# Retention and soft mixture of experts on one core: where the constant tables are fetched, and five warm-up products in place of ten

## The chip, the cores and the metric

The kernel runs on one core of a Trainium2 chip. Its engines each work through a list of their own in order: TensorE (PE; its weight loads are listed as PEld), VectorE (DVE), ScalarE (ACT), GpSimd (POOL) and SyncE (SP), and wait for one another by semaphores. A DMA is issued by an entry of an engine's list (SPq, ACTq) and moved by 16 DMA engines that all queues share. The metric is the device time of one execution in microseconds (us); a table gives the median of several runs. Times inside the kernel are from one profiled execution and count from the start of its span.

## What is computed

Two stages, all in float32. First a retention layer: for 8 batches and 8 heads of 576 positions by 64 features, scores of q and k are weighted by a decay that depends on the head and the distance, without a softmax, and multiplied by v. Then a soft mixture of experts over the 4608 rows of 512 features: logits against 32 slots, a softmax over rows to fill the slots, 8 experts of two layers on 4 slots each, and a softmax over slots to spread the result.

```python
scores = scale * np.matmul(q, k.transpose(0, 1, 3, 2))
gamma = 1.0 - 2.0 ** (-5.0 - np.arange(H, dtype=np.float32))
rel = pos[:, None] - pos[None, :]
Dmat = np.where(rel >= 0, gamma[:, None, None] ** rel[None, :, :], 0.0)
x = np.matmul(scores * Dmat[None, :, :, :], v)        # then (B*S, H*D)
logits = x @ phi
d = np.exp(logits - logits.max(0)); d /= d.sum(0) + 1e-09
slot_input = (d.T @ x).reshape(E, S_per_e, D)
for e in range(E):
    h = np.maximum(slot_input[e] @ w1[e], 0.0)
    slot_out[e] = h @ w2[e]
c = np.exp(logits - logits.max(1)); c /= c.sum(1) + 1e-09
return c @ slot_out
```

## The kernel before

The rows are cut into 36 tiles of 128 (a tile is one batch's 128 positions, all heads; the last 64 positions of two batches share a tile). The main loop runs over tiles `t`. For each there is one load of k and v (`kv`, 512 KB, four buffers) and one of q (`qs`, 256 KB, three buffers); only tile 0 gets k and v in two transfers, with q between them. The order on each engine is the order in which the code is written: `manual_schedule` lets nothing move it.

The steps of a tile, by line:

- `stage_k` (L175, L176): TensorE transposes k in four products, ScalarE copies the result to `kt`. In the loop, `stage_k(t + 1)` stands directly behind `stage_a(t)`.
- `stage_a` (L190; L195, L198): products of `kt` and q into the PSUM tile `pss`; VectorE multiplies them by masks out of the constants `cst` and writes `sT`.
- `scale` (L150, L158): GpSimd multiplies v in place by a column of `cst`, and makes `gb`, the decay table for this chunk, out of the table `g0` and `cst`.
- `stage_i` (L217): adds what earlier chunks left in the running state; the first two tiles have none.
- `stage_c` (L250, L253): k times the scaled v, into the running state.
- `stage_b` (L229, L236): scaled v times `sT` into `px`; VectorE multiplies by `gb`.

TensorE's order around the start is therefore: warm-up, `stage_k(0)`, `stage_a(0)`, `stage_k(1)`, `stage_c(0)`, `stage_b(0)`, `stage_a(1)`, `stage_k(2)` and so on. Tiles are gathered in groups of four for the softmax (L258 and further). The last part (from L566) computes the experts and writes the output.

Ahead of the loop stand the constants and the warm-up. `cst` holds masks and factors, 128 x 380 (190 KB); `g0` is 128 x 512 (256 KB). Both are issued by ScalarE, as its first two entries; SyncE issues the loads of tiles 0 to 3 at the same time, in the order k, q, v of tile 0, then k/v and q of tile 1, k/v and q of tile 2, k/v of tile 3. The warm-up is ten products of a 128 x 128 tile of zeros, `wz`, which VectorE fills first; nobody reads their result. ScalarE loads its activation table ahead of its first compute instruction, which before is the copy L176 of tile 0. `lrun` is a column that the softmax uses from the first group on, where it is first written by L282.

The semaphores of the DMAs are taken in turn, eight of them, so the issue of a later DMA can wait for an earlier one to land. The queue rows in the section on the change show which.

Of the kernel before, what the change touches and what calls it, by code (L numbers as in the profile page):

```python
# [45 lines left out]
def retention_softmoe(ctx, tc, tok, phi, wun, cst, gtab, msel, out):  # L46
    nc = tc.nc
# [25 lines left out]
    cs_ = cpool.tile([P, NCST], F32, name="cst")  # L73
# [4 lines left out]
    g0 = cpool.tile([P, NP, P], F32, name="g0")  # L78
# [7 lines left out]
    lrun = cpool.tile([P, 1], F32, name="lrun")  # L86
# [19 lines left out]
        if t < NT:  # L106
            nc.sync.dma_start(out=qs[t % NQ], in_=tok[t, :, 1024:1536])

    nc.scalar.dma_start(out=cs_, in_=cst)
    nc.scalar.dma_start(out=g0, in_=gtab)  # L110
    K, V = slice(0, 512), slice(512, 1024)
    load_kv(0, K)
    load_q(0)
# [7 lines left out]
    make_identity(nc, ident)  # L121
    wz = gpool.tile([P, P], F32, name="et")
    nc.vector.memset(wz, 0.0)
    pw = ps_x.tile([P, 2, 512], F32, name="px")
    for _ in range(10):
        nc.tensor.matmul(pw[:, 0, 0:P], lhsT=wz, rhs=wz, start=True, stop=True)  # L126

    for z in range(2):
# [347 lines left out]
    for z in range(2):  # L476
# [4 lines left out]
        if z == 0:  # L481
# [3 lines left out]
            out=acc[:, z * 256:(z + 1) * 256], in0=acc[:, z * 256:(z + 1) * 256], scalar=alpha,  # L485
# [293 lines left out]
```

## Time and profile before

| | us |
|---|---|
| median of 3 runs | 234.44 |
| lowest and highest | 233.66, 235.42 |
| profiled execution, its own time | 234.99 |
| span of the profiled execution | 233.2 |

The span goes from the first to the last instruction; the profiled execution's own time has 1.8 us more around it. The profile is read in these views: the page (busy time of each engine as a share of the span; the chain of work that ended last, followed back from the end); the timeline (start, duration, engine, line, operation, what it writes and reads, how often, and in brackets the idle time ahead of it and what ended that); the DMA issues of a stretch of time, with the time from issue to landing; the windows (busy time of engines in each stretch, with the granted TensorE clock, the busy share of the DMA engines and GB/s); the waits. A product in float32 shows as two MATMUL rows (two passes), a transpose as one. The lines themselves stand in the prediction, beside what is read from them.

### The profile page before, as it was taken

What the parts mean: (1) busy time and instruction counts of PE and PEld (TensorE: products, weight loads), DVE (VectorE), ACT (ScalarE), POOL (GpSimd) and SP (SyncE); (2) the same over time, 40 slices, a digit from 0 to 9 for tenths busy, and PEclk for the clock granted to TensorE, in tenths of its full rate; (3) what the DMA queues carried; (4) which work ended last, traced back from release to release, by engine and by line L of the source; (5) the groups of instructions that cost most, each with busy time, mean ns of one, the idle gap of its engine ahead of it and who ended that gap; (6) DMA issues with size and microseconds to landing.
All of it is one profiled execution on the core that took longest, in us unless ns stands there. A gap on an engine that the chain in (4) does not pass through costs nothing.

```text
span 233.2 us, 9102 instructions
## 1 busy us (share of the span) xinstructions
PE 216.9 (93%) x3971; PEld 159.9 (69%) x3971; DVE 131.8 (56%) x302; ACT 82.4 (35%) x198; POOL 62.5 (27%) x72
## 2 busy tenths in 40 slices
PE   8789999999999999999999999999899999999840
PEld 8678868867786886686887787887673235666530
DVE  0466647757646766845866874764664132445750
ACT  2231542442433433352253253254130142344740
POOL 2843423515314233522443441431030010000000
PEclk9999999999999999999999999999999999999995
DMA  6999899799699789889879999888202999997897
GB/s 221 393 390 317 327 350 318 279 333 371 235 337 339 262 307 402 303 266 350 299 273 359 347 366 293 302 280 288 101 0 89 357 412 405 408 393 297 356 404 311
DMA packets 23079, 72.54 MB, mean 311 GB/s; under 512 B 2560, under 2 KB 2944, under 8 KB 23040
## 3 DMA queue, kind: packets, MB, share of 16 engines
q1 hardware_dynamic: 22752, 71.51, 83.7%
q8 instruction: 31, 0.51, 0.9%
q10 hardware_dynamic: 288, 0.46, 0.6%
q14 instruction: 8, 0.07, 0.1%
HBM read 62.52 MB, written 9.44 MB: 309 GB/s over the span
## 4 chain that ended last, share of the span: by engine, by line
PE 87%; DVE 4%; ACT 2%; issue 2%; DMA 1%; DVEq 0%
PE px L229 14%; PE pss L190 13%; PE pn L258 8%; PE pst L250 7%; PE px L217 7%; PE pn L175 7%; PE pm L614 6%; PE pm L272 4%; PE pm L320 4%; PE po L639 3%; PE pst L566 3%; PE pn L566 3%; PE px L126 2%; DVE sT L195 2%; DVE sT L198 1%
## 5 line engine op out<-in xcount | busy, mean ns | idle before, releaser
L150 POOL TENSOR_TENSOR kv<-kv,cst 128x512 f32<-128x512 f32 x36 | 37.6, 1043 | 86.0 <-DMA kv<-in_tok 75.9
L236 DVE TENSOR_TENSOR x<-px,gb 128x512 f32<-128x512 f32 (+1 forms) x37 | 24.9, 675 | 30.9 <-PE px L229 30.7
L229 PE MATMUL px<-sT,kv 128*64 128x128 f32 x576 | 38.6, 275 | 2.7 <-DVE sT L198 1.9
L195 DVE TENSOR_TENSOR sT<-pss,cst 64x256 f32<-64x256 f32 x72 | 30.3, 421 | 11.9 <-PE pss L190 9.4
L176 ACT COPY kt<-pn 128x512 f32<-128x512 f32 x36 | 21.1, 588 | 42.0 <-PE pn L175 42.0
L190 PE MATMUL pss<-qs,kt 64*64 64x64 f32 (+1 forms) x1152 | 32.9, 248 | 1.4 <-ACT kt L176 0.7
L229 PEld LDWEIGHTS px<-sT,kv 128*64 128x64 f32 x576 | 30.9, 137 | 4.7 <-PE pst L250 2.4
L260 ACT COPY x<-pn 128x512 f32<-128x512 f32 x33 | 19.3, 586 | 36.5 <-PE pn L258 36.4
L190 PEld LDWEIGHTS pss<-qs,kt 64*64 64x64 f32 x1152 | 26.4, 133 | 8.4 <-issue 5.8
L250 PEld LDWEIGHTS pst<-kv 128*64 128x64 f32 x512 | 17.5, 137 | 10.1 <-issue 8.1
L175 PE MATMUL pn<-ident,kv 128*128 128x128 f32 x144 | 22.7, 280 | 0.3 <-DMA kv<-in_tok 0.3
L198 DVE TENSOR_TENSOR sT<-pss,cst 128x512 f32<-128x512 f32 x32 | 22.1, 692 | 0.9
L250 PE MATMUL pst<-kv 128*64 128x64 f32 x512 | 21.9, 228 | 0.0
L258 PE MATMUL pn<-ident,x 128*128 128x128 f32 x132 | 21.7, 287 | 0.1
L158 POOL TENSOR_TENSOR gb<-g,cst 128x512 f32<-128x512 f32 x16 | 16.7, 1041 | 12.0 <-DVE x L236 12.0
L217 PE MATMUL px<-qs,sb 64*64 64x128 f32 (+1 forms) x512 | 18.8, 267 | 0.0
L175 PEld LDWEIGHTS pn<-ident,kv 128*128 128x128 f32 x144 | 16.1, 141 | 2.1 <-DMA kv<-in_tok 0.4
L258 PEld LDWEIGHTS pn<-ident,x 128*128 128x128 f32 x132 | 13.8, 140 | 4.5 <-issue 2.8
L253 ACT COPY sb<-pst 128x256 f32<-128x256 f32 x32 | 11.7, 367 | 13.0 <-PE pst L250 12.6
L217 PEld LDWEIGHTS px<-qs,sb 64*64 64x64 f32 x512 | 12.4, 132 | 4.7 <-DVE sT L195 3.4
L601 DVE COPY ws<-po 128x512 f32<-128x512 f32 x15 | 10.1, 690 | 8.4 <-PE po L639 8.3
L599 ACT COPY ws<-po 128x512 f32<-128x512 f32 x15 | 8.7, 589 | 10.5 <-PE po L639 9.5
(143 smaller groups left out, 219.5 us busy)
## 6 DMA issues: line engine op xcount, KB each, us to landing
ws<-in_w SPq DMA_DIRECT2D x61, 512.0 KB, 6.4
kv<-in_tok SPq DMA_DIRECT2D x35, 512.0 KB, 5.5
qs<-in_tok SPq DMA_DIRECT2D x36, 256.0 KB, 4.7
out<-ws SPq DMA_DIRECT2D x14, 512.0 KB, 4.1
kv<-in_w SPq DMA_DIRECT2D x3, 512.0 KB, 4.9
out<-kv SPq DMA_DIRECT2D x3, 512.0 KB, 5.0
kv<-in_tok SPq DMA_DIRECT2D x2, 256.0 KB, 4.0
out<-ws SPq DMA_DIRECT2D x2, 256.0 KB, 6.5
```

The lines of the kernel that those rows point to most:

```text
L150: nc.gpsimd.tensor_tensor(out=v, in0=v, in1=vt[:, c, :].unsqueeze(2).broadcast_to([P, H, D]), op=ALU.mult)
L175: nc.tensor.transpose(pk[:, a, :], k[:, 2 * a:2 * a + 2, :].rearrange("p j d -> p (j d)"), ident)
L176: nc.scalar.copy(out=kt, in_=pk)
L190: nc.tensor.matmul(ps[r, j, a, cols], lhsT=kt[e, a, r], rhs=q[e, a, cols], start=True, stop=True, skip_group_check=True)
L195: nc.vector.tensor_tensor(out=s[r, :, aa, 0:64], in0=ps[r, :, aa, 0:64], in1=tri[r].unsqueeze(1).unsqueeze(2).broadcast_to([D, 2, 2, 64]), ...
L198: nc.vector.tensor_tensor(out=s[:, :, :, 64:P], in0=ps[:, :, :, 64:P], in1=gm.unsqueeze(1).broadcast_to([P, 2, NP, 64]), op=ALU.mult)
L217: nc.tensor.matmul(px[r, j, a // 2, cols], lhsT=sb[i if c == NCH else b % 2][e, a, :], rhs=qT(t)[e, a, cols], start=(i == 0 and a < 2), st ...
L229: nc.tensor.matmul(px[al * D:(al + 1) * D, j, z, :], lhsT=v[:, 2 * a + j, :], rhs=s[:, j, a, :], start=(c == 0 and z == 0), stop=True, ski ...
L236: nc.vector.tensor_tensor(out=xv[:, j], in0=px[:, j, 0:2], in1=g[:, j], op=ALU.mult)
L250: nc.tensor.matmul(pst[j * D:(j + 1) * D, a, :], lhsT=k[:, 2 * a + j, :], rhs=v[:, 2 * a + j, :], start=(c == 0 and a == 0 and b % 2 == 0) ...
L258: nc.tensor.transpose(pn[:, a, :], xT[t][:, a, :], ident)
L260: nc.scalar.copy(out=x, in_=pn)
```

## The change

The two issues of the constants move behind a new ScalarE instruction, a copy of one column of zeros into `lrun`, which waits for VectorE's fill of `wz`. The warm-up has five products in place of ten. Nothing else is changed; line numbers grow by one behind this place.

```diff
-    nc.scalar.dma_start(out=cs_, in_=cst)
-    nc.scalar.dma_start(out=g0, in_=gtab)
     K, V = slice(0, 512), slice(512, 1024)
     load_kv(0, K)
     load_q(0)
...
     wz = gpool.tile([P, P], F32, name="et")
     nc.vector.memset(wz, 0.0)
+    nc.scalar.copy(out=lrun, in_=wz[:, 0:1])
+    nc.scalar.dma_start(out=cs_, in_=cst)
+    nc.scalar.dma_start(out=g0, in_=gtab)
     pw = ps_x.tile([P, 2, 512], F32, name="px")
-    for _ in range(10):
+    for _ in range(5):
         nc.tensor.matmul(pw[:, 0, 0:P], lhsT=wz, rhs=wz, start=True, stop=True)
```

ScalarE at the program's start, before the change (`g_138` is `g0`):

```order
L109 DMA cst<-in_cst 128x380
L110 DMA g_138<-in_gtab 128x512
L176 ACT_TABLE_LOAD
L176 COPY kt<-pn 128x512 [waits PE_49]
L176 COPY kt<-pn 128x512 [waits PE_49,Activation_49]
```

And after it:

```order
L122 ACT_TABLE_LOAD
L122 COPY lrun<-et 128x1 [waits DVE_49]
L123 DMA cst<-in_cst 128x380
L124 DMA g_138<-in_gtab 128x512
L177 COPY kt<-pn 128x512 [waits PE_49]
L177 COPY kt<-pn 128x512 [waits PE_49,Activation_49]
```

The table load is now ScalarE's first entry, and both issues stand behind it and the copy.

SyncE's first issues, before (`kv_87` to `kv_90` are the buffers of k and v, `qs_91` to `qs_93` those of q, `ws` those of weights):

```order
L103 DMA kv_87<-in_tok 128x512
L107 DMA qs_91<-in_tok 128x512
L103 DMA kv_87<-in_tok 128x512
L103 DMA kv_88<-in_tok 128x1024
L107 DMA qs_92<-in_tok 128x512
L103 DMA kv_89<-in_tok 128x1024
L107 DMA qs_93<-in_tok 128x512 [waits DMAHW0_49]
L103 DMA kv_90<-in_tok 128x1024 [waits DMAHW1_49]
L107 DMA qs_91<-in_tok 128x512 [waits DMAHW3_49,DMAHW2_49,PE_49]
L97 DMA ws_96<-in_w 128x1024
L103 DMA kv_87<-in_tok 128x1024 [waits DMAHW4_49,PE_49,Pool_49]
```

And after:

```order
L103 DMA kv_87<-in_tok 128x512
L107 DMA qs_91<-in_tok 128x512
L103 DMA kv_87<-in_tok 128x512
L103 DMA kv_88<-in_tok 128x1024
L107 DMA qs_92<-in_tok 128x512
L103 DMA kv_89<-in_tok 128x1024
L107 DMA qs_93<-in_tok 128x512 [waits DMAHW0_49]
L103 DMA kv_90<-in_tok 128x1024 [waits DMAHW1_49]
L107 DMA qs_91<-in_tok 128x512 [waits DMAHW2_49,PE_49]
L97 DMA ws_96<-in_w 128x1024 [waits DMAHW3_49]
L103 DMA kv_87<-in_tok 128x1024 [waits DMAHW4_49,PE_49,Pool_49]
```

The order of the issues is the same; what has moved is which load a semaphore stands for. Before, `DMAHW0` is taken by `cst`, 1 by k, 2 by `g0`, 3 by q and 4 by v of tile 0; after, 0 by k, 1 by q, 2 by v, 3 by `cst` and 4 by `g0`.

## The prediction

> **What bounds the kernel now.** I read the page first: the busy times and the chain that ended last.
>
> ```profile
> PE 216.9 (93%) x3971; PEld 159.9 (69%) x3971; DVE 131.8 (56%) x302; ACT 82.4 (35%) x198; POOL 62.5 (27%) x72
> ...
> PE 87%; DVE 4%; ACT 2%; issue 2%; DMA 1%; DVEq 0%
> ```
>
> The kernel is bound by TensorE: 93% busy, and 87% of the chain. An edit in the first ten microseconds can therefore only make the same stream of products start earlier or later. So the second view is the timeline of the first 11 us (start, duration, engine, line).
>
> ```profile
> 0.73 0.40 ACTq L109 DMA_DIRECT2D cst<-in_cst  x1
> 0.73 0.38 SPq L103 DMA_DIRECT2D kv<-in_tok  x1
> ...
> 1.05 4.63 PE L126 MATMUL px<-et 128*128 128x128 f32 x20 [1.05 <-DVE et L123]
> 1.16 0.46 ACTq L110 DMA_DIRECT2D g<-in_gtab  x1
> ...
> 1.64 0.90 SPq L103 DMA_DIRECT2D kv<-in_tok  x2
> 1.65 1.28 ACT L176 ACT_TABLE_LOAD   x1 [1.65 <-PEq L768]
> ...
> 5.47 0.67 PE L175 MATMUL pn<-ident,kv 128*128 128x128 f32 x4
> 6.18 0.59 ACT L176 COPY kt<-pn 128x512 f32<-128x512 f32 x1 [3.25 <-PE pn L175]
> 6.68 1.04 POOL L150 TENSOR_TENSOR kv<-kv,cst 128x512 f32<-128x512 f32 x1 [4.66 <-DMA kv<-in_tok]
> ...
> 6.82 0.90 PE L190 MATMUL pss<-qs,kt 64*64 64x128 f32 x32 [0.68 <-ACT kt L176]
> ...
> 7.80 0.88 DVE L195 TENSOR_TENSOR sT<-pss,cst 64x256 f32<-64x256 f32 x2 [6.80 <-PE pss L190]
> 8.00 0.66 PE L175 MATMUL pn<-ident,kv 128*128 128x128 f32 x4 [0.28 <-DMA kv<-in_tok]
> ...
> 8.58 0.69 PE L250 MATMUL pst<-kv 128*64 128x64 f32 x16
> ...
> 8.71 0.69 DVE L198 TENSOR_TENSOR sT<-pss,cst 128x512 f32<-128x512 f32 x1
> ...
> 9.54 1.09 PE L229 MATMUL px<-sT,kv 128*64 128x128 f32 x16 [0.28 <-DVE sT L198]
> ...
> 10.57 0.90 PE L190 MATMUL pss<-qs,kt 64*64 64x128 f32 x32
> ```
>
> The reader should see two things. The k transposes of tile 0 start at 5.47, when the ten warm-up products end, with no wait of their own. And the transposes of tile 1, which stand ahead of L250 and L229 of tile 0 in TensorE's order, wait until 8.00 for a load. When each load lands is the third view: the DMA issues of narrow windows (last column: us from issue to landing), for k, cst, g0, q and v of tile 0, then k/v and q of tile 1.
>
> ```profile
> kv<-in_tok SPq DMA_DIRECT2D x1, 256.0 KB, 3.1
> cst<-in_cst ACTq DMA_DIRECT2D x1, 190.0 KB, 3.3
> ...
> g<-in_gtab ACTq DMA_DIRECT2D x1, 256.0 KB, 4.3
> qs<-in_tok SPq DMA_DIRECT2D x1, 256.0 KB, 4.2
> ...
> kv<-in_tok SPq DMA_DIRECT2D x1, 256.0 KB, 4.9
> ...
> kv<-in_tok SPq DMA_DIRECT2D x1, 512.0 KB, 5.8
> ...
> qs<-in_tok SPq DMA_DIRECT2D x1, 256.0 KB, 6.0
> ```
>
> With issues at 0.73, 0.73, 1.16, 1.17, 1.64, 2.1 and 2.6 they land at 3.8 (k), 4.0 (cst), 5.5 (g0), 5.4 (q), 6.5 (v), 7.9 (k/v of tile 1) and 8.6 (q of tile 1). So k lay ready 1.6 us before its transposes began: the warm-up was the limit there, not the load.
>
> **Five products fewer.** The ten products are 20 passes; passes start from 1.05 and the transposes follow at 5.47, 4.42/20 = 0.22 us a pass. Five products end about 1.05 + 10 x 0.22 = 3.2. By itself this frees 2.2 us of TensorE ahead of the transposes.
>
> **Constants behind the copy.** ScalarE now starts with its table load (0.73 + 1.28 = 2.0) and the one-column copy. No such copy stands in the trace; the bounds are zero and the other one-column instruction of ScalarE:
>
> ```profile
> L285 ACT ACTIVATE alpha<-mrun,negm 128x1 f32<-128x1 f32 x7 | 2.0, 281 | 0.0
> ```
>
> I take 0.2 (nearer to that row). The issue of cst moves from 0.73 to 2.2 and g0 from 1.16 to 2.6: 1.5 us later. The table load is moved, not added; before it was hidden in the 3.25 us that ScalarE idled ahead of L176. With 3.3 and 4.3 us to landing as before, cst lands at 5.5 and g0 at 6.9; with the longest time of the rows above, 6.0, at 8.2 and 8.6. I take the first: cst and g0 shared the engines evenly with k and q (3.3 beside 3.1, 4.3 beside 4.2), so they don't queue behind SyncE's loads. The first readers of cst are L195 on VectorE and L150 on GpSimd; of g0 L158 on GpSimd, behind L150. SyncE's later issues wait on semaphores that are taken in turn: q of tile 2 now waits for k instead of cst (3.4 instead of 4.0), k/v of tile 3 for q instead of k, the first weights for cst and the k/v of tile 4 for g0. The last two stand behind products of tile 0 anyway. I cost these at nothing; q of tile 2 and k/v of tile 3 queue behind the load of tile 1 and are read after 11.
>
> **k, q and v of tile 0.** cst's 190 KB and part of g0 no longer move beside k. The windows of the first transfers (last column: GB/s):
>
> ```profile
> 1.50:3.50 2.00, 2.00 (x11) 2.00 (x11) 0.00 (x0) 1.28 (x1) 0.47 (x2) 1.00 0.82 242
> 3.50:5.25 1.75, 1.75 (x10) 1.75 (x9) 0.00 (x0) 0.00 (x0) 0.00 (x0) 1.00 1.06 388
> ```
>
> At 388 GB/s 190 KB are 0.5 us, so k lands at about 3.35 (bounds: 3.83 as now, 3.3). q would land near 4.3 and v before 6.5. The transposes start at 3.4 instead of 5.47.
>
> **Where the gain stops.** Transposes at 3.4 at the slow pass rate (4 x 0.21 and a drain, about 1.1) to 4.5, L176 to 5.1, L190 from 5.2 to about 6.3 (partly slow, see below), L195 and L198 of VectorE, which took 7.80 to 9.40, now 6.4 to 8.0. sT is 1.4 us earlier. But the transposes of tile 1 still wait for kv of tile 1, and of the bytes ahead of that load none is gone: k, q, v, cst, g0 and its own 512 KB move at the same rate. So it lands at 7.9 again, the transposes stand at 8.00 and L250 at 8.58, as before. L150 of tile 0 ends by 7.6 as v lands no later, so L250 has its operand. Only then does the early sT count: L229 follows L250 at once. Before, it waited 0.28 for sT. **The sum is -0.28 us**; the other 1.1 us turn into a longer wait for the load of tile 1. Bounds of this term: the first 2 us moved 242 GB/s on two queues, 0.75 us short of 388; if one queue alone ramps at half of that and k/v of tile 1 comes 0.4 later, +0.1; if the later constants let it pass and it lands at 7.1 to 7.3 (some 250 KB of their 446 not yet moved by then: 0.6 to 0.8 us at 388 GB/s), L229 follows at 8.6 to 8.8, -0.8.
>
> Does an early start reach the end? TensorE's waits between 10 and 165 us, and GpSimd's scaling of the k/v of tile 4 against its transposes:
>
> ```profile
> PE px L229 <- DVE sT L198: 1.6, 3, 0.6
> PE pss L190 <- issue: 0.7, 2, 0.4
> ...
> 16.40 1.04 POOL L150 TENSOR_TENSOR kv<-kv,cst 128x512 f32<-128x512 f32 x1 [3.36 <-DMA kv<-in_tok]
> ...
> 18.81 0.66 PE L175 MATMUL pn<-ident,kv 128*128 128x128 f32 x4
> ```
>
> No wait for a load is among them, and tile 4's k/v is there 2.4 us ahead: a shift of under 1 us is not eaten. Near the end, with TensorE's last products ahead:
>
> ```profile
> 215.00:217.00 2.00, 1.89 (x10) 1.00 0.69 277
> ```
>
> At 215 the DMA engines are not full (0.69). The outputs that still move after TensorE's end at 224 (its rows stand below) thus start when TensorE delivers, and shift with it.
>
> **The clock, where I had to choose.** The warm-up's passes are longer than the transposes right behind them (ns, minimum, median, maximum; first and last start):
>
> ```profile
> L126 PE MATMUL px<-et x20: 421/421/579, 1.0 to 5.3; 128*128 128x128 f32 x20
> ...
> L175 PE MATMUL pn<-ident,kv x12: 272/273/341, 5.5 to 11.8; 128*128 128x128 f32 x12
> ```
>
> 421 against 273, and starts 0.21 apart against 0.11: the array ran at half rate until about 5.60, though the clock column says 1.00. TensorE's busy time in windows cut there:
>
> ```profile
> 0.99:2.19 1.20, 1.14 (x5) 1.00 0.33 54
> 2.19:5.60 3.41, 3.41 (x18) 1.00 1.03 352
> 5.60:9.01 3.41, 2.46 (x55) 1.00 0.95 363
> ...
> 224.05:227.47 3.42, 0.08 (x1) 1.00 1.02 405
> 227.47:230.88 3.41, 0.00 (x0) 0.50 1.02 405
> ```
>
> The rate rose after a stretch that was full, and fell at 227.47, 65 times 3.413 us later, after an idle one; a stretch of which 1.14 of 3.41 us were busy (33%) did not raise it. In the changed kernel the stretch 2.19 to 5.60 holds the products to 3.3, the transposes to 4.5 and L190 from 5.2: some 2.5 of 3.41 us, 73%. Whether that is enough the trace doesn't show; 73% lies 0.6 of the way from 33 to 100, and I take it that it is. Price if not: L190 at half rate (0.80 becomes 1.6) ends at 6.8, still hidden behind the load; the stretch to 9.01 is 63% busy, so it doesn't raise the clock either; then the transposes from 8.00 to 9.1, L250 1.2 to 10.3, L229 2.0 to 12.3, where now the next product stands at 10.57; the stretch to 12.43 is full. +1.8 us.
>
> The Trainium skill (TensorE: Matmul & The Clock Gate, Part 1: The HAM clock gate) says that the array's clock is released after one busy window of about 3.4 us of sustained activity, that the window runs free, and that the budget is one of time and not of products. The trace agrees on the window (65 of them) and the half rate. Read strictly, the rule speaks against this change: by it five products, 2.1 us, are too few, and the sum would be the +1.8 of the last paragraph instead of -0.28.
>
> **The rivals.**
> - *The clock rises late* (the paragraph above): 234.44 + 1.8 = 236.2. For it: the pauses ahead of 5.2 and, after 6.8, until 8.00. Against it: 73% busy. It decides from the point at which L250 and L229 of tile 0 run at half rate, so slower than before. Were tile 1 slow too, its L190, L250 and L229 would add another 1.5 to 2 and pass 1%.
> - *The constants come late.* L195 and L150 wait for cst; from a landing at 7.8 on each microsecond is lost in full. At 8.2 L150 ends at 9.3, L250 to 9.9, against 9.54 now: +0.4, 234.8. For it: the landing times grew to 6.0 with the queue; against it: the even sharing. The Trainium skill (ScalarE: Activation LUTs, What ACT_TABLE_LOAD costs) adds a drain of 1.38 us to a table load; no row here shows one, since ScalarE idled then. By it cst would land at 6.9, still ahead of 7.8, and the sum stays.
> - *The load of tile 1 comes earlier*, -0.8: 233.6. The late constants speak for it, the unchanged bytes against it.
> - *The change does nothing that can be seen*: the load of tile 1 holds L250 and L229 wherever sT is. It is my forecast less 0.28 us.
>
> **How the numbers follow.** The profiled execution took 234.99 (span 233.2 and 1.8 around it), 0.55 above the median of 234.44 in runs of 233.66 to 235.42; against it the sum gives 234.7, and against the median 234.16, so 234.2. Chances: forecast, with nothing visible, 0.50; clock late 0.30, of which 0.05 past tile 1; constants late 0.08; tile 1's load early 0.12. The range reaches from the early load with a part of the runs' spread (233.6 - 0.3 = 233.3) to the late clock with a little of it (236.3). The likeliest case alone spans 233.6 to 234.9. A measurement of this kernel tells 1%, 2.3 us, from no change: no case gains that much (0.02 for what I haven't seen), and only the clock that stays low past tile 1 loses it (0.05). Same: 0.93.
>
> **What the profile will show.** Right: L126 ends near 3.3, the transposes of tile 0 start near 3.4, sT is done near 8.0, the transposes of tile 1 wait for their load until about 8.0 with a wait of 1 us or more, L229 starts near 9.25 with no wait, and later rows stand 0.3 earlier. L126's 421 ns should be followed by passes of 273 from about 5.6 on. Wrong: L250 and L229 of tile 0 with durations near 420, or L195 or L150 waiting for cst, or the transposes of tile 1 away from 8.0.

## The result and the profile after

| | median, us | runs |
|---|---|---|
| before | 233.86 | 20 (232.17 to 235.78) |
| after | 236.28 | 20 (234.59 to 239.10) |

The ratio is 1.0091, with a 95% interval of 1.0066 to 1.0117: the change costs 2.1 us, 1.5 to 2.7. That is slower by more than the measurement is uncertain, by about 1%. The forecast of 234.2 had the wrong direction; the time lies just under the end of the range, where the rival with the late clock stood. The ratios here and below leave out executions over 1.5% above the fastest of their kernel (three of the 20 after, six of the twelve of e4), so a ratio and its two medians can differ, and in e4 they point apart.

The page of the kernel after, span, busy time, clock, and the chain that ended last:

```profile
span 232.8 us, 9083 instructions
...
PE 215.4 (93%) x3961; PEld 159.0 (68%) x3961; DVE 130.3 (56%) x302; ACT 82.7 (36%) x199; POOL 62.4 (27%) x72
...
PEclk9799999999999999999999999999999999999995
...
PE 85%; DMA 4%; DVE 3%; ACT 2%; issue 1%; SPq 1%; DVEq 0%
```

Two things are new: a 7 in the clock's second slice, and 4% of DMA in the chain. The profiled execution happens to be the fastest of its 20 (234.59), so its span must not be set against 233.2 of before; only the beginning is compared here. The timeline of the kernel after shows it:

```profile
0.73 1.28 ACT L122 ACT_TABLE_LOAD   x1 [0.73 <-PEq L769]
...
1.04 0.41 ACTq L123 DMA_DIRECT2D cst<-in_cst  x1
...
1.05 2.50 PE L127 MATMUL px<-et 128*128 128x128 f32 x10 [1.05 <-DVE et L121]
...
2.02 0.19 ACT L122 COPY lrun<-et 128x1 f32<-128x1 f32 x1
...
3.48 1.09 PE L176 MATMUL pn<-ident,kv 128*128 128x128 f32 x4
...
5.24 0.90 PE L191 MATMUL pss<-qs,kt 64*64 64x128 f32 x32 [0.67 <-ACT kt L177]
...
7.13 0.69 DVE L199 TENSOR_TENSOR sT<-pss,cst 128x512 f32<-128x512 f32 x1
...
8.23 1.08 PE L176 MATMUL pn<-ident,kv 128*128 128x128 f32 x4 [2.08 <-DMA kv<-in_tok]
...
9.23 1.12 PE L251 MATMUL pst<-kv 128*64 128x64 f32 x16
...
10.15 1.82 PE L230 MATMUL px<-sT,kv 128*64 128x128 f32 x16
...
11.89 0.90 PE L191 MATMUL pss<-qs,kt 64*64 64x128 f32 x32
```

Up to 7.8 it goes as forecast: transposes at 3.48, scores at 5.24, sT done at 7.8, and TensorE then waits 2.08 us for the load of tile 1. But the transposes behind the wait take 1.08 in place of 0.66, L251 1.12 in place of 0.69, L230 1.82 in place of 1.09. The products of tile 1 stand at 11.89, before at 10.57: 1.3 us late, not 0.3 early. These long rows of L251 and L230 are the sign that the prediction named for being wrong. The windows of the same kernel, cut where its clock changed (length, TensorE busy, clock, DMA share, GB/s), say why:

```profile
1.48:4.90 3.42, 3.09 (x14) 1.00 0.85 285
4.90:8.31 3.41, 0.98 (x33) 1.00 1.02 354
8.31:11.72 3.41, 3.41 (x36) 0.50 1.03 411
11.72:15.14 3.42, 2.80 (x66) 1.00 0.94 349
```

The clock rose at 4.90, after a window that was 90% busy. The next window, with the wait in it, was 29% busy (0.98 of 3.41), and the whole window behind it ran at half rate: exactly the one with tile 0's last products. This is one phase of the windows; the experiments show others.

### The profile page after: what moved, and what is told of

It is laid out like the page before. It is cut to its first block, busy times and chain, and to the rows that moved or that the text cites. A ratio compares the mean times of both kernels' runs of the same rounds, so it can differ in the third digit from the quotient of the medians.

```text
span 232.8 us, 9083 instructions
## 1 busy us (share of the span) xinstructions
PE 215.4 (93%) x3961; PEld 159.0 (68%) x3961; DVE 130.3 (56%) x302; ACT 82.7 (36%) x199; POOL 62.4 (27%) x72
## 4 chain that ended last, share of the span: by engine, by line
PE 85%; DMA 4%; DVE 3%; ACT 2%; issue 1%; SPq 1%; DVEq 0%
PE px L230 15%; PE pss L191 12%; PE pn L259 8%; PE pst L251 8%; PE pn L176 7%; PE px L218 7%; PE pm L615 6%; PE pm L273 4%; PE pm L321 4%; PE po L640 3%; PE pst L567 3%; PE pn L567 3%; DMA kv<-in_tok 3%; DVE sT L196 1%; DMA out<-ws 1%
## 5 line engine op out<-in xcount | busy, mean ns | idle before, releaser
L230 PE MATMUL px<-sT,kv 128*64 128x128 f32 x576 | 39.3, 279 | 2.4 <-DVE sT L199 1.6
L230 PEld LDWEIGHTS px<-sT,kv 128*64 128x64 f32 x576 | 31.7, 139 | 4.3 <-PE pst L251 2.0
L191 PE MATMUL pss<-qs,kt 64*64 64x64 f32 (+1 forms) x1152 | 31.8, 247 | 0.7 <-ACT kt L177 0.7
L176 PE MATMUL pn<-ident,kv 128*128 128x128 f32 x144 | 23.6, 289 | 2.2 <-DMA kv<-in_tok 2.1
L251 PEld LDWEIGHTS pst<-kv 128*64 128x64 f32 x512 | 17.9, 140 | 10.3 <-issue 8.4
L251 PE MATMUL pst<-kv 128*64 128x64 f32 x512 | 22.4, 231 | 0.0
L254 ACT COPY sb<-pst 128x256 f32<-128x256 f32 x32 | 11.7, 367 | 12.8 <-PE pst L251 12.3
```

The costliest lines, as they stand in the source:

```text
L176: nc.tensor.transpose(pk[:, a, :], k[:, 2 * a:2 * a + 2, :].rearrange("p j d -> p (j d)"), ident)
L191: nc.tensor.matmul(ps[r, j, a, cols], lhsT=kt[e, a, r], rhs=q[e, a, cols], start=True, stop=True, skip_group_check=True)
L230: nc.tensor.matmul(px[al * D:(al + 1) * D, j, z, :], lhsT=v[:, 2 * a + j, :], rhs=s[:, j, a, :], start=(c == 0 and z == 0), stop=True, ski ...
L251: nc.tensor.matmul(pst[j * D:(j + 1) * D, a, :], lhsT=k[:, 2 * a + j, :], rhs=v[:, 2 * a + j, :], start=(c == 0 and a == 0 and b % 2 == 0) ...
```

## The experiments

All times are medians with the ratio to the kernel before, run on the same chip. "Products of zeros" are the warm-up's own, which nobody reads; where a kernel has more of them, only idle products are added.

| run | what | median, us | before, us | ratio, 95% |
|---|---|---|---|---|
| e1 | constants moved, ten products | 234.62 | 233.65 | 1.0040 (1.0001 to 1.0078) |
| e2 | constants first, five products | 235.33 | 233.65 | 1.0083 (1.0050 to 1.0115) |
| e3 | after, and 8 products in the wait | 234.99 | 233.65 | 1.0040 (1.0001 to 1.0078) |
| e4 | after, other order of loads | 234.67 | 233.65 | 0.9969 (0.9923 to 1.0014) |
| e5 | e4 and 2 products | 233.37 | 234.02 | 0.9970 (0.9941 to 0.9999) |
| e6 | after, and 2 + 6 products | 233.13 | 234.02 | 0.9970 (0.9947 to 0.9993) |
| e7 | after, and 2 products | 234.63 | 234.02 | 1.0052 (1.0022 to 1.0082) |
| e8 | before, with 7 + 2 + 4 products | 232.77 | 234.21 | 0.9934 (0.9901 to 0.9968) |
| e9 | after with eight products | 234.67 | 234.21 | 1.0030 (0.9990 to 1.0070) |
| e10 | e8, k of tile 1 ahead | 232.41 | 233.32 | 0.9956 (0.9928 to 0.9983) |
| e11 | e8 once more | 232.96 | 233.32 | 0.9984 (0.9954 to 1.0013) |

**e1 and e2: which half of the change costs.** e1 is the changed kernel with

```diff
-    for _ in range(5):
+    for _ in range(10):
```

> The changed kernel with ten warm-up products again, so the constants' move alone. Theory A (the clock falls, or stays at half rate, because TensorE pauses for the load of tile 1): the transposes of tile 0 start at 5.5 again, the pause shrinks to under 0.5 us, the clock rises once and stays; +0.3 us against before from the later load of tile 1, at most +0.7 as an average over the phase of the clock's windows. Theory B (the moved constants make the loads of tile 1 late, and that is the loss): +1.5 to +2.5, as the whole change.

e2 is the kernel before with

```diff
-    for _ in range(10):
+    for _ in range(5):
```

> The kernel before with five products, the constants first as before. Theory A: transposes of tile 0 at about 3.9, when k lands, a pause of about 1.3 us ahead of the transposes of tile 1; half rate in a part of the executions, +0.7 to +1.3 us against before. Theory B: the load of tile 1 lands at 7.9 as before, so no loss: -0.3 to +0.2.

Measured: e1 +0.4%, 0.0 to 0.8; e2 +0.8%, 0.5 to 1.2. Five products alone, with the constants where they were, cost 1.9 us (1.2 to 2.7), nearly the whole 2.1: the loss does not need the moved constants, so theory B falls as its cause. The move alone is not cleared by this: e1's 0.9 us (0.0 to 1.8) lies between theory A's 0.3 to 0.7 and theory B's 1.5 to 2.5. e2's first stages and windows:

```profile
4.02 1.09 PE L175 MATMUL pn<-ident,kv 128*128 128x128 f32 x4 [0.47 <-DMA kv<-in_tok]
5.78 1.55 PE L190 MATMUL pss<-qs,kt 64*64 64x128 f32 x32 [0.68 <-ACT kt L176]
8.48 1.11 PE L175 MATMUL pn<-ident,kv 128*128 128x128 f32 x4 [1.14 <-DMA kv<-in_tok]
9.52 1.12 PE L250 MATMUL pst<-kv 128*64 128x64 f32 x16
10.43 1.92 PE L229 MATMUL px<-sT,kv 128*64 128x128 f32 x16
```

```profile
0.19:3.61 3.42, 2.50 (x10) 1.00 0.51 152
3.61:7.02 3.41, 2.32 (x36) 1.00 1.02 347
7.02:10.43 3.41, 2.27 (x31) 1.00 1.02 396
10.43:13.85 3.42, 3.42 (x53) 1.00 0.91 338
```

Every product is long here: scores 1.55 us in place of 0.90. Windows 73%, 68% and 67% busy did not raise the clock; it rose at 13.85, after a full one. (The clock column says 1.00 where the trace holds no clock record yet; the durations tell.) In this phase the clock never falls, it rises late.

e1's own profile fell once, after a window with the pause (1.41 of 3.42, 41%), behind a load of tile 1 that came at 9.4:

```profile
2.97:6.38 3.41, 3.41 (x17) 1.00 0.89 285
6.38:9.80 3.42, 1.41 (x36) 1.00 0.98 392
9.80:13.21 3.41, 3.41 (x41) 0.50 1.03 406
```

**e3 and e4: fill the wait, or take it away.** e3 adds to the changed kernel, behind `stage_a(0)`,

```diff
         stage_a(t)
+        if t == 0:
+            for _ in range(8):
+                nc.tensor.matmul(pw[:, 0, 0:P], lhsT=wz, rhs=wz, start=True, stop=True)
```

> The changed kernel with eight more products of zeros (read by nobody) between the scores of tile 0 and the transposes of tile 1. Theory A: the pause of 2.1 us is filled with 1.75 us at full rate, the clock rises once and stays, L251 and L230 of tile 0 run at full rate: 0.0 to +0.4 us against before, so 1.5 to 2 us of the loss are gone. Theory B: +2 stays, or more if the products run past the landing.

e4 changes the order of the loads of the changed kernel:

```diff
-    nc.scalar.dma_start(out=g0, in_=gtab)
...
-    for t in range(1, NQ):
+    load_kv(1, K)
+    nc.sync.dma_start(out=g0, in_=gtab)
+    load_q(1)
+    load_kv(1, V)
+    for t in range(2, NQ):
```

> The changed kernel with another order of loads: k of tile 1 alone (256 KB) directly behind v of tile 0, then g0 on SyncE's queue, q and v of tile 1. Both theories take the load of tile 1 for the next limit: its k should land near 6.0 and v of tile 0 near 5.5, so the pause is gone or under 0.8 us, L230 of tile 0 starts at 8 to 8.5 and the products of tile 1 at 9 to 9.6 in place of 10.57. Theory A: -1.0 to -1.5 us against before, with the clock up once in most phases. Theory B: -1.0 to -1.5 as well; if the clock falls here too, 0 to +1.

Both fell short: e3 gets back about half (+0.4%), and e4 shows no gain, where -0.4 to -0.6% was expected: its ratio is -0.3% with an interval that holds zero, and its median lies 1.0 us above that of before. The windows of e3, then of e4, show what was overlooked:

```profile
0.39:3.80 3.41, 2.54 (x11) 1.00 0.55 177
3.80:7.21 3.41, 2.74 (x37) 1.00 0.87 269
7.21:10.63 3.42, 3.42 (x17) 1.00 1.03 411
```

```profile
0.55:3.97 3.42, 2.90 (x12) 1.00 0.60 198
3.97:7.38 3.41, 2.74 (x39) 1.00 1.00 348
7.38:10.79 3.41, 3.41 (x39) 1.00 1.04 415
```

In both the clock rose only behind the third window, at 10.63 and 10.79: 80% (2.74 of 3.41) and 85% (2.90 of 3.42) do not raise it. The missing share is a hole that neither kernel filled, the 0.7 us in which TensorE waits for ScalarE's copy of k. In e3 the eight products even ran at half rate, 3.8 us, until 10.6, past the landing of tile 1's load at 8.7.

**e5, e6 and e7: fill the hole.** All three add, ahead of the loop,

```diff
     stage_k(0)
+    for _ in range(2):
+        nc.tensor.matmul(pw[:, 0, 0:P], lhsT=wz, rhs=wz, start=True, stop=True)
```

e5 to e4, e7 to the changed kernel, and e6 to the changed kernel with six products behind `stage_a(0)` as in e3.

> The kernel of e4 (other order of loads) with two more products of zeros between the transposes of tile 0 and its scores, where TensorE waited 0.7 us for the copy of k. Theory C (the clock rises only after a window of 3.41 us that TensorE fills to more than 80%, and falls after one filled to less than some 50%): TensorE is now busy without a hole from 1.05 until 7, so the clock rises by 7.4 whatever the phase, and stays. -0.8 to -1.5 us against before, all runs shifted; in the profile no half-rate product after 7.4. If five products and the pauses were not the cause, the two products cost their 0.2 us: 0 to +0.2 against e4.

> The changed kernel with two more products of zeros behind the transposes of tile 0 and six behind its scores: same loads, same order, but TensorE busy without a hole from 1.05 until the load of tile 1. Theory C: the clock rises once, by 7.4, and stays; the loss is gone: -0.2 to +0.4 us against before. If the later loads were the cause, +1.5 to +2 remain.

> The changed kernel with only the two products behind the transposes of tile 0; the pause ahead of the transposes of tile 1 stays. Theory C: the clock rises by 7.4 in every phase, and falls again in those in which a window lies mostly in the pause: +0.8 to +1.5 us against before, between e6 and the changed kernel. If only the rise mattered, as e6; if the two products did nothing, +2.1.

e6 is the clean test: its loads and their order are those of the changed kernel, its TensorE does 2.7 us more idle work (1.06 and 1.60), and the loss is gone: 0.9970, 0.9947 to 0.9993. Its first stages and windows:

```profile
5.44 0.94 PE L191 MATMUL pss<-qs,kt 64*64 64x128 f32 x32
6.31 1.60 PE L360 MATMUL px<-et 128*128 128x128 f32 x12
8.35 0.66 PE L176 MATMUL pn<-ident,kv 128*128 128x128 f32 x4 [0.44 <-DMA kv<-in_tok]
8.94 0.69 PE L251 MATMUL pst<-kv 128*64 128x64 f32 x16
9.45 1.05 PE L230 MATMUL px<-sT,kv 128*64 128x128 f32 x16
10.43 0.90 PE L191 MATMUL pss<-qs,kt 64*64 64x128 f32 x32
```

```profile
2.15:5.56 3.41, 3.39 (x19) 1.00 1.05 335
5.56:8.98 3.42, 2.98 (x50) 1.00 0.91 354
8.98:12.39 3.41, 3.41 (x85) 1.00 1.05 415
```

The clock rises at 5.56 and stays. The transposes of tile 1 still wait for their load, until 8.35, and the scores of tile 1 stand at 10.43, 0.14 ahead of before: the order of size of the forecast's -0.28, which the clock had hidden; e6's interval, -1.2 to -0.2 us, holds that too. e7, with the wait left in, gave +0.5%, between e6 and the change, as expected: in its profile the window with the wait was 2.02 of 3.42 us busy (59%), and the clock held there; by e1 and the kernel after, other phases lose it. So from +0.9% filling the first hole alone leads to +0.5% (e7), filling the wait alone to +0.4% (e3), and only both to -0.3% (e6). e5 gave -0.7 us, just short of the -0.8 to -1.5 that were expected, with an interval of -1.4 to 0.0.

**e8 and e11: the constants first, clock steady.** e8 is the kernel before with seven products in place of ten, two behind `stage_k(0)` and four behind `stage_a(0)`.

> The kernel before, constants first, with seven products, two behind the transposes of tile 0 and four behind its scores: TensorE busy without a hole as in e6, but without the constants' move. Theory C (a window filled to more than 80% raises the clock, one under some 50% lowers it): the clock rises by 7.4 and stays, -0.4 to +0.2 us against before. Set beside e6 it gives what the constants' place is worth when the clock is steady: if nothing, the two agree within 0.4 us; if the move helps by itself, e6 is faster by more.

> The kernel of e8 once more, unchanged, beside e10 on one chip: -0.8 to -1.8 us against before if e8's -1.4 holds; 0 to -0.5 if it was luck of the draw.

0.9934, and 0.9984 when run again: together about -0.4%, the second run not told from no change. So with the constants where they had been the kernel is about as fast as e6: no gain from their move shows. e8's profile has two windows of 3.41 and 3.38 busy us and the clock up from 5.97 on.

**e9: does the loss go with the number of products?** The changed kernel with eight products.

> The changed kernel with eight products in place of five. Theory C: eight fill 1.05 to 4.5, then the pauses follow; a window is filled to over 80% in only a part of the phases, and the later pause can lower the clock again: +1.0 to +2.1 us against before, nearly the whole loss, though three of the five products are back. If the loss goes with the number of products: +0.8 (two fifths of 2.1).

+0.7 us, -0.2 to +1.6: under theory C's +1.0 to +2.1, though the interval reaches into it, and about what a loss in proportion (+0.8) would give. The expectation missed, and says that the shares found here do not settle how often each phase comes. That the number of products alone decides is excluded by e3 and e6: both have thirteen, at +0.4% and -0.3%, in other places. The profile of e9 (an execution of 237.0 us, the slowest of its twelve) does show the mechanism: the window with the wait of tile 1 was 30% busy, the clock fell, and the next window, 86% busy, raised it again:

```profile
5.56:8.97 3.41, 1.03 (x33) 1.00 0.96 369
8.97:12.39 3.42, 2.94 (x30) 0.50 1.05 415
12.39:15.80 3.41, 2.79 (x66) 1.00 0.72 256
```

**e10: a version that is faster than both.** e8 with the loads of tile 1 cut as in e4 (`load_kv(1, K)`, `load_q(1)`, `load_kv(1, V)`, constants first) and two products in place of four behind `stage_a(0)`.

> The kernel of e8 with the k of tile 1 as a load of its own ahead of q and v of tile 1, and two products in place of four behind the scores of tile 0. The k of tile 1 lands at about 7.2 in place of 7.9, the transposes of tile 1 start at 7.3, L229 of tile 0 waits for sT until 8.7 in place of 9.2: 0.3 to 0.5 us under e8, -1.3 to -2.0 us against before. If the load of tile 1 were no limit any more, as e8.

0.9956, 0.9928 to 0.9983, the lowest median of all (232.41, 0.9 us under before and 0.55 under e11). Less than expected, but faster than before and than the change. Its runs and those of e11 overlap, so that cutting the load helps on top of e8 is not shown.

## Why the prediction was wrong

- *Five products fewer; k, q and v of tile 0*: right. The transposes were forecast at 3.4 and came at 3.48, sT at 8.0 and came at 7.8. But k landed at 3.3, as forecast, although the constants had moved far less than the forecast assumed (next point): its reason for that landing holds at most in part, and the agreement is partly luck.
- *Constants behind the copy*: wrong, without effect. I moved their issue behind the table load and the copy, to 2.2. It came at 1.04, while the table load ran from 0.73 to 2.0 and the copy started at 2.02. Here ScalarE's list did not hold the DMA issue until the work ahead of it was done; the time fits the copy's wait for VectorE's fill, which ended at 1.00 (0.83 + 0.17). So cst was issued 0.3 us later, not 1.5, and landed no later than before (3.9 and 4.0).
- *Where the gain stops*: right in kind. The load of tile 1 is the next limit, at 8.23 and not 8.00, inside the bound given. The 2.08 us wait was forecast as harmless waiting. It was not, by the next point.
- *The clock, where I had to choose*: this step failed. I took a window 73% busy as enough, since 73 lies nearer to 100 than to 33. So the sum had nothing for the clock, where the measured loss, 2.1 us, goes with the clock. Windows of 67, 68, 73, 74, 80 and 85% did not raise the clock (e2, e3, e4); those of 86, 90 and more did (e9, the kernel after, and the full ones). Filling TensorE through both holes, with nothing else changed, took the loss away (e6 against the change). I also asked only whether the clock rises, not whether the longer wait lowers it again: windows of 29, 30 and 41% did (after, e9, e1), 59 and 72% did not (e7, before). And I laid the windows of before's profile (2.19 to 5.60) over the changed kernel, though windows that run free needn't start there: in the profile after they stood at 1.48 and 4.90, the first was 90% busy, and the loss there came from the fall alone.
- *The rival "the clock rises late"*: +1.8 was its price, 2.1 (1.5 to 2.7) is the measured loss, and its mechanism is the measured one, in the late rise (e2's profile, where tile 1's scores start at 12.28 against the 12.3 worked out there, and are slow as well) and in a second form that it did not name, the fall (the profile after). That its 236.2 meets the 236.28 so closely is luck: it started from 234.44, the median of three runs, where that of 20 is 233.86. I gave it 0.30. What spoke for it was in the text: the strict reading of the Trainium skill (TensorE: Matmul & The Clock Gate, Part 1: The HAM clock gate), one busy window of about 3.4 us of sustained activity, the budget one of time and not of products. The runs agree with it: "sustained" means here more than 80% of the window, since two windows of 80% did not raise the clock. I set the rule aside for a straight line between two shares, which no row supported.
- *The constants come late* and *the load of tile 1 comes earlier*: neither happened. The load of tile 1 landed at 8.2 to 9.4 in the six profiles with the moved constants and that load whole (after, e1, e3, e6, e7, e9), against 7.9 to 8.4 in the four with the constants first (before, e2, e8, e11). So it tends to come later, which lengthens the very wait that lets the clock fall, and e1's loss may come from there; why it does is open. With the holes filled, e6 against e8 and e11, the intervals put the place of the constants between a gain of 0.5 us and a loss of 1.0.
- *An early start reaches the end*: this held. In the six experiments' profiles in which TensorE, from 10 us on, never stops without a wait that the profile shows (e5, e11, e6, e3, e2, e1), the scores of tile 2 start at 13.25, 13.83, 14.18, 16.38, 16.69 and 16.80, and the spans are 229.4, 230.8, 231.3, 233.9, 233.1 and 234.1: a start some 3 us later is an end some 3 us later. A single pair of profiles can hide it. The kernel after is 1.3 us behind before at 15 us and 0.4 us ahead at 163 (last full tile, before, then after):

```profile
163.84 1.04 PE L229 MATMUL px<-sT,kv 128*64 128x128 f32 x16
```

```profile
163.43 1.05 PE L230 MATMUL px<-sT,kv 128*64 128x128 f32 x16
```

Between them before's execution lost 1.7 us more, 1.4 of it around 58 and 64 us, in stops like those of the last section. They differ between two executions of one kernel: e8's profile has one of 0.32 us at 135, e11's has none. What part of the spread of 20 runs, 3.6 us, is theirs and what part the phase of the clock's windows was not measured; either way only medians carry the sum.

## What to carry to other kernels

Idle products at the start bought the clock here, so their number is right when TensorE is busy without a hole from the first one until the real stream runs dense; shortening them because the data come sooner can cost more than it saves, when a copy or a load then opens a hole. Ask for each wait near the start not only who waits, but how full it leaves the window of 3.41 us around it, for every phase of the windows. A wait that can't be removed is worth filling with products that nobody reads: here eight of them turned +0.9% into -0.3%.

## What the runs showed of the hardware

- TensorE's clock changes on a grid of 3.413 us whose phase differs from run to run: first rises such as those at 4.90, 5.56, 5.60, 5.97, 6.38, and at 10.63 to 13.85 where the first windows were not full.
- The busy share of a window that raises the clock lies between 80 and 90% (one window of 85% did not, one of 86% did; TensorE's ends are modelled and the two held different work, so the border is not known that finely). The share that keeps it lies between 41 and 59%.
- Transposes counted as busy: without them the window of the kernel after that raised the clock would be about 60% busy and that of e9 56%, where e4's first window has 73% without them and did not raise it.
- TensorE can stop in the midst of a run of products with nothing that the profile shows it waiting for, and a long stop lowered the clock too. Timeline and windows of e10's profiled execution, which took 237.8 us where the median was 232.4:

```profile
45.37 0.44 PE L193 MATMUL pss<-qs,kt 64*64 64x128 f32 x7
48.24 1.12 PE L193 MATMUL pss<-qs,kt 64*64 64x64 f32 x21 [2.43 <-issue]
```

```profile
44.54:47.95 3.41, 1.27 (x23) 1.00 0.80 273
47.95:51.36 3.41, 3.12 (x34) 0.50 0.92 350
```

Before's profile has short ones of the same kind:

```profile
58.38 0.56 PE L190 MATMUL pss<-qs,kt 64*64 64x128 f32 x13 [0.39 <-issue]
```

The pages list a DMA queue of instructions (q8: 31 packets, 0.51 MB after as before), in a mean traffic of some 310 GB/s. Whether a late packet of it is what stops TensorE was not tried and stays open.
